# A decode block's last row: the second norm taken from moments, and the last chunks of the row before moved

## The chip, the cores and the metric

The kernel runs on one core of a Trainium2 chip. The metric is the device time of one execution in microseconds (us), as the median of several runs. A profiled execution gives a trace of every engine beside it: TensorE (PE, with its weight loads as PEld), VectorE (DVE), ScalarE (ACT), GpSimd (POOL) and SyncE (SP), which issues the transfers.

## The reference

A decode step for B = 4 rows of D = 512 channels: adaptive layer norm, cached attention with 32 query heads over 8 key heads, and a token-mixing MLP, each behind a gate.

```python
x = A_x
mod = (_silu(c) @ w_mod).reshape(c.shape[0], 6, 1, -1)
sa, ca, ga, sb, cb, gb = (mod[:, 0], mod[:, 1], mod[:, 2], mod[:, 3], mod[:, 4], mod[:, 5])
h = _layernorm(x, axis=-1) * (1 + ca) + sa
x = x + ga * _A_ref(h, A_k_cache, A_v_cache, A_wq, A_wo)   # softmax attention over 4096 cached keys
h = _layernorm(x, axis=-1) * (1 + cb) + sb
x = x + gb * _B_ref(h, B_w1, B_b1, B_w2, B_b2)

# _B_ref, with S = 1 token and F = 1792 features
h = _layernorm(x, axis=-1)
u = _gelu(jnp.einsum("bsd,sf->bdf", h, w1) + b1)
y = jnp.einsum("bdf,fs->bds", u, w2) + b2
```

So between the attention's output and the gelu of one row stand two layer norms in sequence: the modulated one, h1 = norm(x) * (1 + cb) + sb, and a second, plain norm of h1 inside `_B_ref`. Then each of 1792 features takes gelu(norm(h1) * w1 + b1), and the features are summed with w2.

## The kernel before

The 32 pairs of row and key head are worked through in order, pair i being row i // 8. Each has 2 MB of keys and 2 MB of values, which SyncE's queue loads into a ring of three 4 MB slots. For pair i `scores` multiplies, `row_max` to `expo` make the softmax's numerators, `turn` transposes them, `values` multiplies by the values, `pick` and `copy_o` bring the head's output into columns and `project` multiplies it by its part of wo. The sum over the heads is a row's attention output. The MLP of a row, class `Mixer`, runs under the attention of the next row: its 14 chunks of 128 features are expanded (`expand`, on VectorE), put through gelu on ScalarE and contracted with w2 on TensorE, two chunks at a time. A row is held in a folded form, [128 partitions, 128 columns]: partition group c of 32 holds the channels c*128 to c*128 + 127, and 8 partitions of each group belong to one row. The gates and shifts lie in `prep` in the same form.

For the last pairs the order of all steps is written out by hand in the string `PLAN`, whose words are read from left to right; each engine executes its own instructions in that order. `mix` is the MLP of row 2 there: `x` expands its next two chunks, `g` is their gelu, `c` contracts one such pair of chunks. Words with capital or small letters and a number are steps of a pair (`V29` copies the values' product of pair 29, `P28` adds the projection of pair 28, `p31` projects pair 31, `E` forms what the last row has besides its last two heads). `T2` and `T3` touch the root and the gelu on ScalarE ahead of their use, so that the function table is loaded there.

The words that begin with z are the last row's own path. Its attention output with the residual is summed in PSUM, in `pgx[:, 4]`; the mean `mu` is known shortly before. `zs` squares the centred row on ScalarE and sums it per partition, `za` (`centre`) multiplies the centred row by 1 + cb on VectorE, `zq` sums over the partitions on TensorE, `zm` (`adaln_last`) takes the root, forms h1 up to a factor and takes its statistics, `zb0` and `zb1` broadcast h1 to all partitions by matmuls, two of its four groups each, `zv` (`gather_more`) brings the statistics together, and `zn` (`affine`) takes the mean and the variance from them, the power -1/2 on GpSimd, a copy `hb` of the broadcast row less its mean on ScalarE, and the weights `wr` times the power. `zc` closes row 2's contraction, which is 512 columns wide and accumulates in four groups of partitions. `finish` then runs the last row's 14 chunks: the first two by ScalarE alone, the others expanded by VectorE, all through gelu on ScalarE and contracted on TensorE; the outputs follow.

Of the kernel before, what the change touches and what calls it, by code (L numbers as in the profile page):

```python
# [10 lines left out]
OP = mybir.AluOpType  # L11
# [17 lines left out]
def adaln_decode(ctx: ExitStack, tc: tile.TileContext, small, x, wmod, wq, kk, kv, vv, wo, out):  # L29
# [64 lines left out]
    osb = cst.tile([P, B, P], F32, name="osb")  # L94
# [95 lines left out]
    def load_wm5():  # L190
        t = slots().rearrange("p s (k n) -> p (s k) n", n=D)
        nc.sync.dma_start(t[:, 0:4], wmod[2][:, 1])
        WM[5] = t[:, 0:4]
        return t[:, 4:6]
# [178 lines left out]
    XK = cst.tile([P, B, P], F32, name="xk")  # L373
# [34 lines left out]
    def centre(x, mu):  # L408
        a = wk.tile([P, P], F32, name="a")
        dv.scalar_tensor_tensor(a, x, mu, prep[:, 3], op0=OP.add, op1=OP.mult)  # L410
        return a

    def adaln_last(b, pst, a):
        r = cst.tile([P, 1], F32, name="sd")
        h1 = wk.tile([P, P], F32, name="h1")
        nc.scalar.activation(r, pst, AF.Sqrt, bias=epsc, scale=1.0 / D)
        dv.scalar_tensor_tensor(h1, prep[:, 2], r, a, op0=OP.mult, op1=OP.add)
        pst = ps_m.tile([P, 27], F32, name="pst", tag="m")
        dv.tensor_scalar(pst[:, 24:27], eps9, r, r, op0=OP.mult, op1=OP.mult)
        return h1, stats(h1, b), pst  # L420

# [28 lines left out]
    def contract_wide(py, u, js):  # L450
        for e, j in enumerate(js):
            q = j % 4
            mm(py[32 * q:32 * q + 32, :], w2[:, j:j + 1].to_broadcast([P, 32]), u[:, e, :],  # L453
               start=(j < 4), stop=(j >= NF - 4))

    class Mixer:
# [21 lines left out]
        def gather_more(self):  # L478
            mm(self.pst[:, 0:24], ones, self.st.rearrange("p a b -> p (a b)"), start=True, stop=True)
            self.st = self.pst  # L480

        def modulate(self):
            if self.b < B - 1:
                self.h1, self.st = adaln(self.b, self.st)
            else:
                self.h1, self.st, self.pst = adaln_last(self.b, self.st, self.a)
# [26 lines left out]
        def consume(self, most=9):  # L513
            if self.py is None:
                self.py = ps_e.tile([P, D if self.wide else P], F32, name="py", tag="e")
            for u, js in self.done[:most]:
                (contract_wide if self.wide else contract)(self.py, u, js)
# [34 lines left out]
    def finish(b, pg, py, hb, wr):  # L552
        uu = ring.tile([P, 16, D], F32, name="uu", tag="kv")
        for js in ((0,), (1,), (2, 3, 4), (5, 6, 7), (8, 9, 10), (11, 12), (13,)):
# [17 lines left out]
        dv.scalar_tensor_tensor(gx, gbl, b2, XK[:, b], op0=OP.mult, op1=OP.add)  # L572
# [15 lines left out]

    def fold_gate(gate, es):
# [7 lines left out]
    mu = cst.tile([P, 1], F32, name="mu")  # L597

# [19 lines left out]
    for i in range(NS - HKV):  # L618
# [30 lines left out]
        if i == 2:  # L649
            for t in range(2, 5):  # L650
# [11 lines left out]
    mix, row = Mixer(B - 2), Mixer(B - 1)  # L662
    pve = pgx = pc = ep = spare = slot = None
# [9 lines left out]
    b31 v28.1 B31 f e31 LV31 l30 V28 L30 t30.1 l31 L31 a28 t31.1 A28 p28 v29.0 v29.1 t30.0 f P28 V29 v30.0 a29  # L673
    v30.1 A29 LW p29 f v30.2 v30.3 t31.0 P29 g V30 Y y a30 A30 p30 E x v31.0 f v31.1 v31.2 v31.3 V31 z31 a31 I A31 j p31
    g T2 zs za zx zq c c zm zb0 T3 zv zb1 zw0 zn zc
# [5 lines left out]
           "N": mix.normalise, "g": mix.gelu, "c": lambda: mix.consume(1), "zc": mix.gather_up, "zv": row.gather_more,  # L681
           "zg": row.gather,
           "zm": row.modulate, "zn": lambda: row.normalise(cst.tile([P, 1], F32, name="yl"))}
    for step in PLAN.split():
# [25 lines left out]
        elif op == "LW":  # L710
            spare = load_wm5()
        elif op == "x":
            mix.expand(spare if mix.n == 6 else None)
# [18 lines left out]
        elif step == "T3":  # L732
            nc.scalar.activation(tab, neg1, AF.Gelu_apprx_tanh)
        elif op == "zq":
            ph = ps_s.tile([P, 8, P], F32, name="ph3", tag="s")
            row.st = ph[:, 2, 0:1]
            mm(row.st, g32[:, 8 * (B - 1):8 * (B - 1) + 1].to_broadcast([P, P]), sq, start=True, stop=True)
        elif op == "zs":
            sq = cst.tile([P, 1], F32, name="sq")
            flat = wk.tile([P, P], F32, name="flat")  # L740
            nc.scalar.activation(flat, pgx[:, 4], AF.Square, bias=mu, accum_out=sq)
        elif op == "j":
            tally_up()
        elif op == "za":
            row.a = centre(pgx[:, 4], mu)
        elif op == "zx":
            dv.tensor_copy(XK[:, B - 1], pgx[:, 4])
        elif op == "zw":
            modmm(pgx[:, 0], 5, (0,))
        elif op == "zb":  # L750
            if i:
# [37 lines left out]
```

## Time and profile before

| | |
|---|---|
| time, median of 3 runs | 386.73 us (386.31 to 386.73) |
| span of the profiled execution | 384.7 us (its own time isn't listed) |
| mean granted TensorE clock | 0.883 |
| PE busy | 298.7 us, 78% |
| DVE busy | 198.2 us, 52% |
| ACT busy | 112.2 us, 29% |
| DMA, whole span | 157.69 MB, 410 GB/s |

The span runs from the first to the last instruction of the profiled execution; the time holds what lies around it as well. Busy shares are means over the whole span, so a short stretch with another limit has to be read from its own rows.

### The profile page before, as it was taken

The numbers are of one execution on the slowest core, as the hardware profiler recorded it, in microseconds if no ns is written. First come the engines' busy times: TensorE is split into PE (matmuls) and PEld (weight loads), VectorE is DVE, ScalarE is ACT, GpSimd is POOL, SyncE is SP. The second block draws the span as 40 slices with busy tenths as digits, with TensorE's granted clock in tenths as the row PEclk, the third lists the DMA queues.
The fourth block names the chain that finished last, engine by engine and source line by source line (L and its number), as shares of the span: only waits on it lengthen the run. The fifth ranks groups of instructions, "written<-read, shape, count | busy, mean of one in ns | idle before, by whom it ended". The sixth has DMA issues, their size and how long they took to land.

```text
span 384.7 us, 5604 instructions
## 1 busy us (share of the span) xinstructions
PE 298.7 (78%) x2380; PEld 117.2 (30%) x2380; DVE 198.2 (52%) x407; ACT 112.2 (29%) x144; POOL 7.7 (2%) x33
## 2 busy tenths in 40 slices
PE   0856777866966949979877878788888887999984
PEld 0112122311323313334322222342222343333653
DVE  1130251620451424664866545557665567778757
ACT  1001111121110110212567311124575105657276
POOL 1100000000000000000000000000000000000000
PEclk9989555985695685998999998999999999999999
DMA  8999999999999999999999999999999999999930
GB/s 331 433 433 436 411 453 433 409 432 436 423 441 433 434 436 436 434 436 431 429 425 433 428 433 434 429 433 431 429 434 436 434 436 432 424 417 423 418 122 3
DMA packets 7409, 157.69 MB, mean 410 GB/s; under 512 B 964, under 2 KB 1236, under 8 KB 1496
## 3 DMA queue, kind: packets, MB, share of 16 engines
q1 hardware_dynamic: 7376, 157.33, 95.4%
q8 instruction: 18, 0.29, 0.3%
q14 instruction: 7, 0.06, 0.0%
q10 hardware_dynamic: 8, 0.00, 0.0%
HBM read 157.32 MB, written 0.01 MB: 409 GB/s over the span
## 4 chain that ended last, share of the span: by engine, by line
DMA 60%; PE 29%; DVE 7%; ACT 2%; issue 1%; POOL 0%; SPq 0%; POOLq 0%; DVEq 0%
DMA kv<-in_kv 58%; PE s L231 8%; PE pv L291 7%; PE s L122 2%; PE qs L138 2%; DVE m L236 2%; DVE p L267 2%; DMA sm<-in_small 2%; PE pa L343 2%; PE pt L328 2%; ACT uu L562 1%; PE pb L251 1%; PE pve L303 1%; PE pm L240 1%; PE pgx L348 1%
## 5 line engine op out<-in xcount | busy, mean ns | idle before, releaser
L231 PE MATMUL s<-kv,QT 128*32 128x512 f32 x512 | 75.2, 714 | 38.9 <-DMA kv<-in_kv 37.0
L236 DVE TENSOR_REDUCE m<-s 128x1 f32<-128x1024 f32 x32 | 39.2, 1224 | 96.0 <-PE s L231 95.9
L261 ACT ACTIVATE p<-s,nm 128x1024 f32<-128x1024 f32 x32 | 35.7, 1115 | 180.6 <-DVE nm L256 180.5
L291 PE MATMUL pv<-kv,p 128*32 128x512 f32 x464 | 69.8, 670 | 0.7 <-DMA kv<-in_kv 0.7
L231 PEld LDWEIGHTS s<-kv,QT 128*32 128x32 f32 x512 | 15.8, 123 | 84.0 <-DMA kv<-in_kv 52.5
L328 PEld LDWEIGHTS pt<-g,po 128*128 128x128 f32 x236 | 31.1, 205 | 27.2 <-issue 19.9
L343 PE MATMUL pa<-wo,oT 128*32 128x512 f32 x240 | 34.6, 648 | 4.6 <-DVE oT L335 4.4
L328 PE MATMUL pt<-g,po 128*128 128x4 f32 (+2 forms) x236 | 33.9, 267 | 1.5 <-DVE po L314 1.0
L267 DVE STREAM_TRANSPOSE p<-p 128x1024 f32<-128x1024 f32 x25 | 30.9, 1234 | 0.0
L314 DVE COPY po<-pv 128x512 f32<-128x512 f32 x29 | 20.0, 688 | 16.8 <-PE pv L291 16.7
L245 DVE TENSOR_REDUCE mx<-pm 1x128 f32<-1x512 f32 x32 | 21.3, 669 | 1.1 <-PE pm L240 1.1
L442 DVE TENSOR_SCALAR u<-hb,wr,sm 128x512 f32<-128x512 f32 x40 | 19.9, 541 | 1.9 <-POOL wr L437 1.0
L506 ACT ACTIVATE u<-u 128x1024 f32<-128x1024 f32 x20 | 20.4, 1051 | 1.5 <-DVE u L442 1.4
L361 DVE TENSOR_TENSOR acc<-acc,pa 128x512 f32<-128x512 f32 x26 | 17.8, 686 | 4.3 <-PE pa L343 4.2
L261 ACT ACT_TABLE_LOAD x11 | 14.1, 1283 | 20.3 <-DVE nm L256 20.2
L251 PEld LDWEIGHTS pb<-neg,mx 1*128 1x128 f32 x64 | 10.4, 202 | 28.2 <-DVE mx L245 26.5
L122 PE MATMUL s<-wm,sT 128*4 128x512 f32 x16 | 9.1, 732 | 10.6 <-DVE sT L108 10.6
L506 ACT ACT_TABLE_LOAD x13 | 16.7, 1283 | 0.2
L291 PEld LDWEIGHTS pv<-kv,p 128*32 128x32 f32 x464 | 13.4, 146 | 7.2 <-issue 3.1
L240 PE MATMUL pm<-ident,m 128*1 128x128 f32 x32 | 9.3, 289 | 7.4 <-DVE m L236 3.5
L251 PE MATMUL pb<-neg,mx 1*128 1x1 f32 x64 | 13.1, 271 | 2.1 <-DVE mx L245 2.1
L453 PE MATMUL py<-u,sm 128*32 128x512 f32 x80 | 14.4, 616 | 0.0
(158 smaller groups left out, 214.7 us busy)
## 6 DMA issues: line engine op xcount, KB each, us to landing
kv<-in_kv SPq DMA_DIRECT2D x28, 4096.0 KB, 21.9
wq<-in_wq SPq DMA_DIRECT2D x2, 4096.0 KB, 16.3
wo<-in_wo SPq DMA_DIRECT2D x4, 2048.0 KB
kv<-in_kv SPq DMA_DIRECT2D x4, 2048.0 KB, 20.3
wm<-in_wmod SPq DMA_DIRECT2D x2, 2048.0 KB, 14.8
kv<-in_kk SPq DMA_DIRECT2D x1, 4096.0 KB
kv<-in_vv SPq DMA_DIRECT2D x3, 1024.0 KB
wm<-in_wmod SPq DMA_DIRECT2D x1, 1024.0 KB
```

The source lines that it names most:

```text
L231: mm(s[32 * c:32 * c + 32, n * 512:(n + 1) * 512], QT[:, b, h, :], KT[i][:, (n * 4 + c) * 512:(n * 4 + c + 1) * 512], start=True, stop=True)
L236: dv.tensor_reduce(M[i], S[i], axis=AX.X, op=OP.max)
L245: dv.tensor_reduce(mx, M[i].rearrange("o (c r) -> o r c", c=4).unsqueeze(1).to_broadcast([1, 4, 32, 4]), axis=AX.X, op=OP.max)
L251: mm(pb, M[i].rearrange("o c r -> o (c r)"), neg1, start=True, stop=True)
L261: nc.scalar.activation(p, S[i], AF.Exp, bias=M.pop(i), accum_out=l)
L267: dv.transpose(PL[i][0], PL[i][0])
L291: mm(PV[i][32 * q:32 * q + 32, :], pT[:, 128 * k:128 * k + 128:4], VT[i][:, 4 * k:4 * k + 4, :].rearrange("p j d -> p (j d)"), start=(k < ...
L314: dv.tensor_copy(PV[i], pv)
L328: mm(pt, po[:, c * DH:(c + 1) * DH], sel.unsqueeze(1).to_broadcast([P, m, REP]), start=(c == 0), stop=(c == n - 1))
L343: mm(pa[32 * g:32 * g + 32, :], oT[:, g:g + 1].to_broadcast([P, 32]), wo_t[h][:, g, :], start=True, stop=True)
L442: dv.tensor_scalar(u[:, e, :], hb, wr[:, j:j + 1], b1[:, j:j + 1], op0=OP.mult, op1=OP.add)
L506: nc.scalar.activation(u, u, AF.Gelu_apprx_tanh)
```

## The change

The last row's second norm is no longer taken from h1. With a = (x - mean) * (1 + cb) and the shift sb, h1 is a / sd + sb, so the variance of h1 follows from four sums over the row: of the squares of x - mean, of a, of a squared and of a times the centred shift. `zs` and `last_rows` sum the first two, `zp` and the second reduction of `last_rows` the other two, all into columns of one small tile `mom`; `zq` and `zv` each bring two of them to all partitions with the constant column `mid`. What depends on the shift alone is made once, early in the stream, by `spread_shift`. The broadcast `zb0`, `zb1` takes a, not h1, so it stands ahead of the root in the order; `hb` is formed behind it on VectorE from a, the root and the broadcast shift. The mean of h1 is not taken off `hb`: it goes, times w1, into the bias of the gelu (`shift`, which stands in for b1 in `finish`).

Row 2's last two pairs of chunks move: the expansion of chunks 12 and 13 and the gelus of 10 to 13 stand ahead of `V29`, beside a copy by ScalarE (`lift`) of the first ten chunks' contraction out of PSUM. In the tail `fold_rest` folds that copy and adds the last four chunks' contraction in narrow form. The last row stays in PSUM (`x1`) instead of `XK`, and `osb` takes a buffer of the pool of the chunks.

```diff
-    v30.1 A29 LW p29 f v30.2 v30.3 t31.0 P29 g V30 Y y a30 A30 p30 E x v31.0 f v31.1 v31.2 v31.3 V31 z31 a31 I A31 j p31
-    g T2 zs za zx zq c c zm zb0 T3 zv zb1 zw0 zn zc
+    b31 v28.1 B31 f e31 LV31 l30 V28 L30 t30.1 l31 L31 a28 t31.1 A28 p28 v29.0 v29.1 t30.0 f P28 g x g zy V29 v30.0 a29
+    v30.1 A29 LW p29 f v30.2 v30.3 t31.0 P29 V30 Y y a30 A30 p30 E v31.0 f v31.1 v31.2 v31.3 V31 z31 a31 I A31 j p31
+    T2 zs za zp zq zb0 zk T3 zv zb1 zn zw0 zc
...
-    eps9 = cst.tile([P, 3], F32, name="eps9")
-    nc.gpsimd.memset(eps9, 0.0)
-    nc.gpsimd.memset(eps9[:, 0:1], 1e-20)
-    nc.gpsimd.memset(eps9[:, 2:3], EPS * D)
+    mid = cst.tile([P, 1], F32, name="mid")
+    dv.tensor_scalar(mid, g32[:, 8 * (B - 1):8 * (B - 1) + 1], 1.0 / D, None, op0=OP.mult)
...
+        def lift(self):
+            self.yw = up.tile([P, 2, D], F32, name="u")[:, 0]
+            nc.scalar.activation(self.yw, self.py, AF.Copy)
+
+        def fold_rest(self):
+            py = ps_e.tile([P, P], F32, name="pc", tag="e")
+            for c in range(4):
+                mm(py[32 * c:32 * c + 32, :], g32, self.yw[:, c * P:(c + 1) * P], start=True, stop=False)
+            for u, js in self.done:
+                for e, j in enumerate(js):
+                    for c in range(4):
+                        mm(py[32 * c:32 * c + 32, :], w2[:, j:j + 1].to_broadcast([P, 32]),
+                           u[:, e, c * P:(c + 1) * P], start=False, stop=(j == NF - 1))
+            self.py = py
...
+    def spread_shift():
+        psb = ps_m.tile([P, 4, P], F32, name="psb", tag="m")
+        for c in range(4):
+            e = 32 * c + 8 * (B - 1)
+            mm(psb[:, c, :], ident[:, e:e + 1].to_broadcast([P, P]), prep[:, 2], start=True, stop=True)
+        psb = psb.rearrange("p c n -> p (c n)")
+        st = wk.tile([P, 6], F32, name="st")
+        dv.bn_stats(st, psb)
+        dv.bn_aggr(smv, st)
+        dv.tensor_scalar(sfull, psb, smv[:, 0:1], None, op0=OP.subtract)
+        dv.tensor_scalar(spart, prep[:, 2], smv[:, 0:1], 2.0, op0=OP.subtract, op1=OP.mult)
+        dv.tensor_scalar(smv[:, 1:2], smv[:, 1:2], EPS, None, op0=OP.add)
...
+    def last_rows(x):
+        al = wk.tile([P, P], F32, name="a")
+        ju = wk.tile([P, P], F32, name="flat")
+        dv.scalar_tensor_tensor(al, x, mu, prep[:, 3], op0=OP.add, op1=OP.mult, accum_out=mom[:, 1:2])
+        dv.tensor_tensor_reduce(ju, al, spart, 1.0, 0.0, OP.mult, OP.add, mom[:, 3:4])
+        return al
+
+    def squares(x, col, **kw):
+        flat = wk.tile([P, P], F32, name="h1")
+        nc.scalar.activation(flat, x, AF.Square, accum_out=mom[:, col:col + 1], **kw)
+
+    def means(dst, cols):
+        mm(dst, mid.to_broadcast([P, P]), mom[:, cols], start=True, stop=True)
+
+    def first_moments(g1):
+        nc.scalar.activation(sd, g1[:, 0:1], AF.Sqrt, bias=epsc)
+        dv.tensor_copy(momc, g1)
+        dv.tensor_scalar(kk1[:, 0:1], momc[:, 0:1], EPS, smv[:, 1:2], op0=OP.add, op1=OP.mult)
+        dv.scalar_tensor_tensor(kk1[:, 1:2], momc[:, 1:2], momc[:, 1:2], kk1[:, 0:1], op0=OP.mult, op1=OP.subtract)
+        dv.tensor_scalar(shift[:, 0], w1, momc[:, 1:2], -1.0, op0=OP.mult, op1=OP.mult)
+
+    def second_moments(g2, ab):
+        y = cst.tile([P, 1], F32, name="yl")
+        wr = wk.tile([P, NF], F32, name="wr")
+        hb = wk.tile([P, D], F32, name="hb")
+        dv.scalar_tensor_tensor(vv1[:, 0:1], g2[:, 1:2], sd, kk1[:, 1:2], op0=OP.mult, op1=OP.subtract)
+        dv.tensor_add(vv1[:, 1:2], g2[:, 0:1], vv1[:, 0:1])
+        root(vv1[:, 1:2], P, y)
+        dv.scalar_tensor_tensor(hb, sfull, sd, ab, op0=OP.mult, op1=OP.add)
+        dv.scalar_tensor_tensor(shift[:, 1], shift[:, 0], y, b1, op0=OP.mult, op1=OP.add)
+        nc.gpsimd.tensor_tensor(wr, w1, y.to_broadcast([P, NF]), op=OP.mult)
+        return hb, wr, shift[:, 1]
...
+        elif op == "zs":
+            squares(pgx[:, 4], 0, bias=mu)
+        elif op == "za":
+            al = last_rows(pgx[:, 4])
+        elif op == "zp":
+            squares(al, 2)
         elif op == "zq":
             ph = ps_s.tile([P, 8, P], F32, name="ph3", tag="s")
+            means(ph[:, 2, 0:2], slice(0, 2))
+        elif op == "zk":
+            first_moments(ph[:, 2, 0:2])
+        elif op == "zv":
+            means(ph[:, 3, 0:2], slice(2, 4))
+        elif op == "zn":
+            hb, wr, b1l = second_moments(ph[:, 3, 0:2], ph[:, 4:8].rearrange("p c n -> p (c n)"))
+            py = ps_v.tile([P, P], F32, name="py3", tag="pv")
...
+            bcast(al, B - 1, ph[:, 4 + 2 * i:6 + 2 * i], (2 * i, 2 * i + 1))
+    finish(B - 1, pgx[:, 0], py, hb, wr, b1l, pgx[:, 4])
```

## Rows read from the trace of the kernel before

**Rows 1.** The page's span in 40 slices: DMA busy tenths, GB/s.

```profile
DMA  8999999999999999999999999999999999999930
GB/s 331 433 433 436 411 453 433 409 432 436 423 441 433 434 436 436 434 436 431 429 425 433 428 433 434 429 433 431 429 434 436 434 436 432 424 417 423 418 122 3
```

**Rows 2.** Chain of waits, end: start, length in us, engine, tile, line.

```profile
370.83 0.99 PE py L453 x8
...
373.88 1.52 ACT uu L557 x2
375.40 4.12 ACT uu L562 x3
...
380.61 0.99 PE py L447 x24
```

**Rows 3.** Timeline, 369.9 to 379.5 us: start, length, engine, line, operation, [idle before].

```profile
369.94 0.37 ACT L741 ACTIVATE flat<-pgx,mu 128x128 f32<-128x128 f32 x1 [1.07 <-PE pgx L348]
370.20 0.19 ACT L741 ACTIVATION_READ_ACCUMULATOR flat<-pgx,mu 128x1 f32 x1
370.43 0.35 DVE L410 SCALAR_TENSOR_TENSOR a<-pgx,mu,prep 128x128 f32<-128x128 f32 x1 [0.77 <-ACT flat L741]
...
370.45 0.38 PE L737 MATMUL ph<-sq,g 128*128 128x1 f32 x2 [0.58 <-ACT flat L741]
...
370.87 0.26 ACT L416 ACTIVATE sd<-ph,epsc 128x1 f32<-128x1 f32 x1 [0.47 <-PE ph L737]
371.15 1.28 ACT L733 ACT_TABLE_LOAD   x1
...
371.94 0.18 DVE L380 TENSOR_TENSOR stm<-st,ident 128x24 f32<-128x24 f32 x1
372.20 0.30 PEld L479 LDWEIGHTS pst<-stm,ones 128*128 128x128 f32 x2
...
372.45 0.69 PE L427 MATMUL py<-h,ident 128*128 128x128 f32 x4
...
373.00 0.55 POOL L100 TENSOR_TENSOR yl<-mv,half 128x1 f32<-128x1 f32 x1 [54.02 <-DVE mv L396]
...
373.61 0.43 PE L366 MATMUL pc<-yw,g 128*32 128x128 f32 x8
373.63 0.21 POOL L437 TENSOR_TENSOR wr<-w1n,yl 128x14 f32<-128x14 f32 x1
...
373.89 5.57 DVE L442 TENSOR_SCALAR uu<-hb,wr,sm 128x512 f32<-128x512 f32 x12 [0.42 <-POOL wr L437]
```

**Rows 4.** Timeline, 358 to 368 us: around row 2's last chunks.

```profile
358.65 0.69 DVE L361 TENSOR_TENSOR acc<-acc,pa 128x512 f32<-128x512 f32 x1
...
360.40 0.29 DVE L314 COPY po<-pvn 128x128 f32<-128x128 f32 x1 [1.06 <-PE pvn L303]
...
364.90 0.35 DVE L726 CUSTOM_DVE_ANT_0 ep<-ep,prep,g 128x128 f32<-128x128 f32 x1
365.17 0.08 DVE L726 DVE_READ_ACCUMULATOR2_ANT tally<- 128x1 f32 x1
365.27 1.00 DVE L442 TENSOR_SCALAR kv<-hb,wr,sm 128x512 f32<-128x512 f32 x2
...
367.23 0.14 PEld L303 LDWEIGHTS pve<-kv,p 128*32 128x32 f32 x4 [0.17 <-DMA kv<-in_vv]
```

**Rows 5.** Groups by form, VectorE: line, operation, count | busy us, mean ns | idle before.

```profile
L361 DVE TENSOR_TENSOR acc<-acc,pa 128x512 f32<-128x512 f32 x26 | 17.8, 686 | 4.3 <-PE pa L343 4.2
...
L256 DVE COPY nm<-pb 128x1 f32<-128x1 f32 x32 | 5.0, 156 | 16.1 <-PE pb L251 16.0
...
L576 DVE TENSOR_TENSOR osb<-py,gbl 128x128 f32<-128x128 f32 x1 | 0.3, 292 | 0.1
```

**Rows 6.** Stretch 88 to 90 us: us, PE, PEld, DVE, ACT, POOL busy, clock, DMA.

```profile
88.00:90.00 2.00, 1.16 (x12) 0.41 (x16) 0.00 (x0) 0.67 (x2) 0.00 (x0) 0.50 0.87 377
```

**Rows 7.** Timeline, the small matmuls in that stretch.

```profile
88.44 0.66 PE L221 MATMUL pc<-ym,g 128*32 128x128 f32 x8 [0.78 <-ACT ym L218]
```

More of the change, by code (lines that the diff above doesn't have):

```diff
@@ L371, in residual @@
         dv.tensor_add(x1, x1, prep[:, 0])
-    XK = cst.tile([P, B, P], F32, name="xk")
+    XK = cst.tile([P, B - 1, P], F32, name="xk")
     ZK = cst.tile([P, B - 1, P], F32, name="zk")
@@ L453, in contract_wide @@
             mm(py[32 * q:32 * q + 32, :], w2[:, j:j + 1].to_broadcast([P, 32]), u[:, e, :],
-               start=(j < 4), stop=(j >= NF - 4))
+               start=(j < 4), stop=(last - 4 < j))
     class Mixer:
@@ L476, in gather @@
             self.pst = None
-        def gather_more(self):
-            mm(self.pst[:, 0:24], ones, self.st.rearrange("p a b -> p (a b)"), start=True, stop=True)
-            self.st = self.pst
         def modulate(self):
[L483 to L486, printed above, removed]
+            self.h1, self.st = adaln(self.b, self.st)
         def spread(self, pb=None, cs=range(4)):
@@ L516, in consume @@
             for u, js in self.done[:most]:
-                (contract_wide if self.wide else contract)(self.py, u, js)
+                if self.wide:
+                    contract_wide(self.py, u, js, NF - 1 if self.b < B - 2 else 9)
+                else:
+                    contract(self.py, u, js)
             del self.done[:most]
@@ L597, in adaln_decode @@
     mu = cst.tile([P, 1], F32, name="mu")
+    smv = cst.tile([P, 2], F32, name="smv")
+    sfull = cst.tile([P, D], F32, name="sfull")
+    spart = cst.tile([P, P], F32, name="spart")
+    mom = cst.tile([P, 4], F32, name="mom")
+    momc = cst.tile([P, 2], F32, name="momc")
+    sd = cst.tile([P, 1], F32, name="sd")
+    kk1 = cst.tile([P, 2], F32, name="kk1")
+    vv1 = cst.tile([P, 2], F32, name="vv1")
+    shift = cst.tile([P, 2, NF], F32, name="shift")
+    def last_rows(x):
[26 more added lines that the diff above has]
+        return hb, wr, shift[:, 1]
     def tally_up():
@@ L656, in adaln_decode @@
                     nc.scalar.activation(dst, pm, AF.Copy)
+        if i == 5:
+            spread_shift()
         if i == NS - HKV - 2:
             gate = spread_gate()
-    mix, row = Mixer(B - 2), Mixer(B - 1)
-    pve = pgx = pc = ep = spare = slot = None
+    mix = Mixer(B - 2)
+    pve = pgx = pc = ep = slot = None
     gates = list(range(2 * REP))
@@ L680, in adaln_decode @@
     MIX = {"F": mix.fold, "R": mix.residual, "G": mix.gather, "M": mix.modulate, "H": mix.gather, "Q": mix.spread,
-           "N": mix.normalise, "g": mix.gelu, "c": lambda: mix.consume(1), "zc": mix.gather_up, "zv": row.gather_more,
-           "zg": row.gather,
-           "zm": row.modulate, "zn": lambda: row.normalise(cst.tile([P, 1], F32, name="yl"))}
+           "N": mix.normalise, "g": mix.gelu, "c": lambda: mix.consume(1), "zy": mix.lift, "zc": mix.fold_rest, }
     for step in PLAN.split():
@@ L710, in adaln_decode @@
         elif op == "LW":
-            spare = load_wm5()
+            load_wm5()
         elif op == "x":
-            mix.expand(spare if mix.n == 6 else None)
+            mix.expand()
         elif op == "f":
@@ L750, in adaln_decode @@
         elif op == "zb":
-            if i:
-                py = ps_v.tile([P, 4, P], F32, name="py3", tag="pv")
-            row.spread(py[:, 2:4] if i else ph[:, 4:6], (2 * i, 2 * i + 1))
-    finish(B - 1, pgx[:, 0], py[:, 0], row.hb, row.wr)
+            bcast(al, B - 1, ph[:, 4 + 2 * i:6 + 2 * i], (2 * i, 2 * i + 1))
+    finish(B - 1, pgx[:, 0], py, hb, wr, b1l, pgx[:, 4])
 def kernel(**inputs):
```

44 lines of the change are left out of this document (10 added, 34 removed).

## Prediction

> **What bounds the kernel now.** I read the page's slices first. The DMA engines are full from the first slices to the one before the last two, at a nearly even rate, and then stop [rows 1]: the kernel streams the caches until about 367 us, and whatever changes before that moment is hidden as long as it neither starves the stream nor delays the work on its last piece. The span is 384.7 us, so some 17 us are a tail without transfers, and only there can this edit earn or lose time. The profiled execution has no time of its own listed; I set its span beside the median of 386.73, which leaves 2.0 us around it, and apply the shift of the span to the median.
>
> Next the chain of waits in the tail [rows 2]. From 373.88 to 381.6 it is ScalarE's gelu of the last row and the last contraction: ScalarE runs without a gap from its first gelu to its last, and VectorE's expansions start together with it [rows 2, 3]. Nothing in this stretch is changed by the edit but its start. So the question is one number: when can the first gelu of the last row start? Before, that is 373.88.
>
> Last the timeline between the end of the row's sum (pgx, about 369.9) and 373.88 [rows 3]. Before, the steps are: square and its accumulator read on ScalarE, a reduction over partitions on TensorE (`zq`), the root, `h1`, its statistics, a second reduction (`gather_more`), mean and variance, the power on GpSimd, the scaled weights, the gelu.
>
> **The change part by part.**
>
> *Ahead of the tail.* Chunk pair 12, 13 of row 2 is expanded before `V29` instead of after `E`: two instructions, 1.00 us [rows 4]. VectorE ended `P28` at 359.34 and then idled 1.06 us until it could copy `V29` at 360.40 [rows 4]; the pair fits in this gap, so I take nothing. What is queued behind it is `V29`, then `A29` and the projection. If the gap were gone the price is up to 1.00 us, less the 0.17 us that TensorE's loads wait for the last piece at 367.23 [rows 4]. Two gelus and the new copy `lift` go to ScalarE, which has nothing else until the tail. `spread_shift`, the constant `mid` and the three memsets lie where DMA is full; no queue that issues transfers waits on them for more than a fraction of a transfer, so nothing either way. No transfer is added, dropped or reordered, and SP and GpSimd's queue are not passed.
>
> *First half of the tail, a loss.* `zs` starts as before and its accumulator read ends at 370.39 [rows 3]. `za` follows at 370.43: it already stood there, with pgx long finished and ScalarE reading the same tile [rows 3]. New is that `zq` reads two sums, so it also waits for `za`'s. With the accumulator read I price `za` by the reduction with a read on the same 128x128, 0.35 and 0.08 overlapping, ending 0.35 after its start [rows 4]: 370.80 with a few hundredths for the start of the next. Below: 0.35, no read. Above: ScalarE's read, 0.19 more [rows 3]. `zq` then begins at 370.86 against 370.45 and ends at 371.24. Meanwhile `zp`, another square with its read, occupies ScalarE from 370.84 for 0.45 to 371.29, so the root `sd` starts at 371.31 and ends at 371.57, against 370.87 and 371.13: **0.44 us later**. The gelu table follows the root in both; its load of 1.28 and the small activation of about 0.2 end near 373.1 and bind nothing.
>
> *Second half, a gain.* After the root the old kernel needs 373.88 - 371.13 = 2.75 us. The new one: `momc` copies the two means out of PSUM, 0.16 by the row of a 128x1 copy [rows 5], from 371.60 to 371.76. `zv` writes into the bank that the root and `momc` read, so TensorE waits for `momc`. Its load begins at 371.83 (old: 372.20, 0.08 after the end of its input [rows 3]). `zb1` is queued behind it. In the old kernel the same pair of jobs, reduction and two broadcasts, took from 372.20 to 373.14, 0.94 us [rows 3]; so the broadcast is complete at 372.77. `hb` on VectorE, 128x512 with one operand in PSUM, is not in the trace. The add of that size is 0.686, and the three-operand form costs 0.352 against 0.292 at 128 columns [rows 3, 5], so I take 0.75: 372.81 to 373.56. Below it is 0.69, the add; above it is four times the 128-column row, 1.41. `shift` is a small instruction behind it, about 0.2, started while `hb` drains: 373.68. The first gelu starts at **373.72**.
>
> Beside it runs the branch over GpSimd. The four small instructions after `momc` are 0.16 to 0.2 each with 0.04 between (bounds: the 128x1 copy, and 0.35 of the 128-column form [rows 3, 5]); the variance stands at about 372.72, the power takes 0.55 and the weights 0.21 with 0.08 ahead of each [rows 3]: about 373.65. So the two branches end nearly together, and speeding up one alone would earn little.
>
> *The old wide contraction* (0.99 us on the chain [rows 2]) leaves the stretch between `zq` and the broadcasts. It is worth less than it looks: behind it waited broadcasts whose input was ready only after the root. `fold_rest` puts 8 and 32 small matmuls after `zw0`. By 0.43 for eight [rows 3] they take no more than 2.2 us, from about 373.2 to 375.4 at the latest. The first contraction of the last row may wait for them, but its sum is needed only at the end; `close` reads them at 379. Removing the copies of pgx and of `yw` on VectorE touches no instruction that the chain waits on.
>
> *Sum.* +0.44 for the later root, then 373.72 - 371.57 = 2.15 instead of 2.75: -0.60. Together **-0.16 us**, a span of about 384.5 us. From the median: 386.73 - 0.16 = 386.57, which I round to **386.5**. With `hb` at 0.69 and no accumulator read, and the GpSimd branch as floor, it is -0.35; with `hb` at 1.41, +0.5.
>
> *One rule against the row.* The order of `zv` behind `momc` is the dearest assumption. The row that bears on it is `za`: pgx was summed at about 369.9, ScalarE began at 369.94, and VectorE, idle, began its read of the same tile only at 370.43, as soon as ScalarE was done [rows 3]. The Trainium skill, PSUM — Partial Sum Buffer, section "PSUM bank collisions raise a hardware error", says that two engines must be kept from one bank and quadrant at the same time even at different columns. By that rule the sum above stands, and this change pays for it three times (`za` behind `zs`, `momc` behind the root, `zv` behind `momc`); without it the sum is that of the first rival.
>
> **The rivals.**
>
> *`zv` is not held.* Its columns are not those that `momc` reads. It could then go as soon as `zp`'s sum stands and `zb0` has passed, about 371.65; the broadcast is done at 372.6, `hb` at 373.38 and the gelu starts at 373.5, a time of 386.73 - 0.37 = 386.4. For it: different columns. Against it: `za`'s start [rows 3].
>
> *The sums share a tile and are taken one after another (slower).* The four columns of `mom` are written by two engines in turn. If the tile, not the column, is what is waited on, `zp` waits for VectorE's second reduction (370.80 + 0.37), and `zq` for `zp`. The root then starts at 372.14 instead of 371.31, +0.83, and the whole is +0.67: 387.4. It decides as soon as the added wait exceeds 0.16 us. Against it: ScalarE and VectorE begin to write different columns of `uu` at 373.88 and 373.89, side by side [rows 2, 3].
>
> *TensorE's clock falls in the tail.* TensorE has less to do from 369.9 to 372. Between 88 and 90 us, granted 0.50 (1.2 GHz), eight of the small matmuls took 0.66; in the tail they took 0.43 at full clock (2.4 GHz) [rows 3, 6, 7]. The last contraction, 0.99 [rows 2], would grow by half, +0.5: 386.73 - 0.16 + 0.5 = 387.1. Against it: old and new both leave a gap after pgx, and the added contraction keeps TensorE busy from 371.8 to 375.
>
> *The moved pair is in the way (slower).* If `P28` ends later, `V29` slips by up to 1.00, and with 0.17 to spare at the last piece the sum is +0.83 - 0.16: 387.4. Against it: what follows from `V29` is folded only at `y`, and the projections of pairs 30 and 31, which come last, do not read it.
>
> **How the numbers follow.** The forecast, with its own range of 386.2 to 386.9, gets 0.62. `zv` not held: 0.09. The shared tile 0.08, the clock 0.06, the moved pair 0.05. I leave 0.10 to shares that I can't see, as a different end of the stream, of either sign. A measurement of this kernel tells about 0.2% from no change, 0.77 us: below 385.96 is faster, above 387.50 slower. The forecast and all the named rivals lie inside; outside reach their edges and the unseen share. Faster 0.12, same 0.80, slower 0.08. The range takes in `zv` not held with `hb` at its cheapest and a little more below, and the shared tile above: 385.8 to 387.3, which leaves out the two dearest cases at their full price.
>
> **What would show it.** In the changed kernel: first gelu of the last row near 373.7 if the stream ends at the same moment; the root about 0.4 later than before, and `zq` starting right after `za`'s accumulator read; TensorE's load for `zv` starting right after `momc`; `hb` near 0.75; `V29` still at 360.4; a copy and two gelus on ScalarE between 357 and 363; granted clock 1.00 to the end. The prediction is wrong if the stream ends at another time, if `zp` or `zq` waits on the second reduction, if `zv` starts before `momc`, or if the stretch after the first gelu is not the 8 us that it was.

## The result, and the profile after

The changed kernel takes 387.9 us, the median of six runs (387.51 to 388.32), against 386.73 (386.31 to 387.87) for the kernel before on the same chip: a ratio of 1.0034, with a 95% interval of 1.0024 to 1.0044. It is slower by some 1.2 us where the forecast was a gain of 0.2, and it lies outside the range that I gave.

The page of the kernel after, its span and the line of the 40 slices that answers to [rows 1]:

```profile
span 386.0 us, 5673 instructions
...
DMA  8999999999999999999999999999999999999910
```

The stream is as full as before; the span has grown from 384.7 to 386.0. The profiled execution took 387.94, so what lies around the span is 1.9 us here too. The whole difference is in the span.

Where in the span? The stretch from the first gelu of the last row to the end of the last add was 8.36 us before (373.88 to 382.24; the last add, from the timeline of the kernel before, 373 to 386 us) and is 8.39 now (375.22 to 383.61, below).

```profile
381.95 0.29 DVE L577 TENSOR_TENSOR osb<-osb,a 128x128 f32<-128x128 f32 x1
```

The row's sum came 0.13 later: `zs` started at 370.07 instead of 369.94 [rows 3]. TensorE's load for the last piece of the stream was as much later, 367.38 for 367.23 [rows 4]; in three of the executions below, with the same stream, it came between 367.05 and 367.40, so I take this as scatter. What is left lies between `zs` and the first gelu. I call this **the stretch**: 369.94 to 373.88 before, 3.94 us; now 370.07 to 375.22, 5.15 us. The forecast had it at 3.78.

The timeline of the kernel after, 353 to 386 us in the first two lines and the last, 369 to 387 in the others (columns as in [rows 3]):

```profile
359.22 1.00 DVE L424 TENSOR_SCALAR u<-hb,wr,sm 128x512 f32<-128x512 f32 x2
...
360.36 0.29 DVE L310 COPY po<-pvn 128x128 f32<-128x128 f32 x1
...
370.07 0.37 ACT L624 ACTIVATE h<-pgx,mu 128x128 f32<-128x128 f32 x1 [6.72 <-PE pgx L344]
...
370.56 0.35 DVE L618 SCALAR_TENSOR_TENSOR a<-pgx,mu,prep 128x128 f32<-128x128 f32 x1 [0.77 <-ACT h L624]
370.83 0.08 DVE L618 DVE_READ_ACCUMULATOR a<-pgx,mu,prep 128x1 f32 x1
370.95 0.31 ACT L624 ACTIVATE h<-a 128x128 f32<-128x128 f32 x1 [0.43 <-DVE a L618]
...
370.97 0.38 PE L627 MATMUL ph<-mom,mid 128*128 128x2 f32 x2 [0.97 <-DVE a L618]
...
371.22 0.69 PE L409 MATMUL ph<-a,ident 128*128 128x128 f32 x4
371.95 0.26 ACT L630 ACTIVATE sd<-ph,epsc 128x1 f32<-128x1 f32 x1 [0.59 <-PE ph L409]
...
372.24 0.16 DVE L631 COPY momc<-ph 128x2 f32<-128x2 f32 x1 [0.99 <-ACT sd L630]
...
372.45 0.38 PE L627 MATMUL ph<-mom,mid 128*128 128x2 f32 x2 [0.55 <-DVE momc L631]
...
372.70 1.05 PE L409 MATMUL ph<-a,ident 128*128 128x128 f32 x4
...
373.78 0.22 DVE L640 SCALAR_TENSOR_TENSOR vv<-ph,sd,kk 128x1 f32<-128x1 f32 x1 [0.73 <-PE ph L409]
...
374.11 0.73 DVE L643 SCALAR_TENSOR_TENSOR hb<-sfull,sd,ph 128x512 f32<-128x512 f32 x1
...
375.22 1.52 ACT L550 ACTIVATE uu<-hb,shift,wr 128x512 f32<-128x512 f32 x2 [1.50 <-POOL wr L645]
...
383.32 0.29 DVE L571 TENSOR_TENSOR u<-u,a 128x128 f32<-128x128 f32 x1
```

Read it for what ends each wait. `zq` starts right behind `za`'s accumulator read, at 370.97, and is done at 371.35. The root (L630) reads nothing but `zq`'s two columns and does not start then: it starts at 371.95, and the wait of 0.59 ahead of it was ended by the matmuls of line 409, the broadcast `zb0`, which end at 371.91. The same happens below: the variance (L640) reads `zv`'s columns, done at 372.83, and starts at 373.78, behind the second broadcast `zb1`, which ends at 373.75. Neither reader uses a broadcast. They share only its tile: `zq` writes `ph[:, 2]`, `zv` `ph[:, 3]`, `zb0` and `zb1` `ph[:, 4:8]`. The trace also holds the counts (semaphores) that one engine raises and the others wait for. TensorE's rises at 371.92 and 373.76, at the ends of `zb0` and `zb1`, and at no time near 371.35: `zq` raises none of its own.

A second thing is in the length of `zb1`, 1.05 where `zb0` took 0.69. The stretches of one microsecond in the kernel after, and the first of them in the kernel before (columns as in [rows 6]):

```profile
373.00:374.00 1.00, 1.00 (x12) 0.76 (x15) 0.26 (x2) 0.71 (x2) 0.00 (x0) 0.50 0.00 0
...
375.00:376.00 1.00, 1.00 (x24) 0.94 (x20) 0.88 (x3) 0.78 (x2) 0.10 (x1) 0.50 0.00 0
```

```profile
373.00:374.00 1.00, 0.88 (x18) 0.34 (x16) 0.58 (x2) 0.92 (x3) 0.76 (x2) 1.00 0.00 0
```

TensorE's granted clock was 0.50 (1.2 GHz) from about 373 to 376, where the kernel before had 1.00 (2.4 GHz). So there were two suspects, the shared tile and the clock, and a third that the trace spoke against already: the moved chunks fit into their gap, as forecast (359.22 to 360.22, and `V29` at 360.36).

### The profile page after: what moved, and what is told of

The parts are those of the page before. It is cut to its first block, busy times and chain, and to the rows that moved or that the text cites. A ratio compares the mean times of both kernels' runs of the same rounds, so it can differ in the third digit from the quotient of the medians.

```text
span 386.0 us, 5673 instructions
## 1 busy us (share of the span) xinstructions
PE 303.0 (78%) x2412; PEld 122.3 (32%) x2412; DVE 200.7 (52%) x417; ACT 112.2 (29%) x145; POOL 7.5 (2%) x30
## 4 chain that ended last, share of the span: by engine, by line
DMA 54%; PE 34%; DVE 8%; ACT 2%; issue 1%; POOL 0%; SPq 0%; POOLq 0%; DVEq 0%
DMA kv<-in_kv 52%; PE s L227 9%; PE pv L287 9%; PE pa L339 3%; DVE m L232 3%; PE pt L324 2%; PE s L119 2%; PE qs L135 2%; DVE p L263 2%; DMA sm<-in_small 2%; PE pb L247 1%; ACT uu L555 1%; PE pve L299 1%; PE pm L236 1%; PE pgx L344 1%
## 5 line engine op out<-in xcount | busy, mean ns | idle before, releaser
L287 PE MATMUL pv<-kv,p 128*32 128x512 f32 x464 | 71.3, 684 | 0.6 <-DMA kv<-in_kv 0.6
L324 PEld LDWEIGHTS pt<-g,po 128*128 128x128 f32 x236 | 32.7, 214 | 27.8 <-issue 18.0
L339 PE MATMUL pa<-wo,oT 128*32 128x512 f32 x240 | 36.3, 679 | 4.1 <-DVE oT L331 4.0
L324 PE MATMUL pt<-g,po 128*128 128x4 f32 (+2 forms) x236 | 35.5, 274 | 1.5 <-DVE po L310 1.0
L481 ACT ACTIVATE u<-u 128x1024 f32<-128x1024 f32 x21 | 21.4, 1051 | 3.8 <-DVE u L424 3.7
L424 DVE TENSOR_SCALAR u<-hb,wr,sm 128x512 f32<-128x512 f32 x42 | 20.9, 540 | 1.9 <-POOL wr L419 1.0
L236 PEld LDWEIGHTS pm<-ident,m 128*1 128x1 f32 x32 | 2.5, 79 | 37.8 <-DVE rl L276 27.4
```

The costliest lines, as they stand in the source:

```text
L287: mm(PV[i][32 * q:32 * q + 32, :], pT[:, 128 * k:128 * k + 128:4], VT[i][:, 4 * k:4 * k + 4, :].rearrange("p j d -> p (j d)"), start=(k < ...
L324: mm(pt, po[:, c * DH:(c + 1) * DH], sel.unsqueeze(1).to_broadcast([P, m, REP]), start=(c == 0), stop=(c == n - 1))
L339: mm(pa[32 * g:32 * g + 32, :], oT[:, g:g + 1].to_broadcast([P, 32]), wo_t[h][:, g, :], start=True, stop=True)
L481: nc.scalar.activation(u, u, AF.Gelu_apprx_tanh)
```

## The experiments

All kernels but one start from the changed kernel; the kernel before ran on the same chips, with medians of 386.48 to 386.52. On one of them (the kernels with only the first and only the second result apart, the short fillers and the shorter second half) its times scattered, from 386.33 to 391.25 about a median of 386.48. That pulls the ratios there down and widens their intervals, so for these kernels I go by the medians.

**Own tiles for both results.** `zq`'s and `zv`'s means go into PSUM tiles of their own; the broadcasts keep `ph`.

```diff
-            means(ph[:, 2, 0:2], slice(0, 2))
+            g1 = ps_m.tile([P, 2], F32, name="g1", tag="m")
+            means(g1, slice(0, 2))
...
-            first_moments(ph[:, 2, 0:2])
+            first_moments(g1)
...
-            means(ph[:, 3, 0:2], slice(2, 4))
+            g2 = ps_m.tile([P, 2], F32, name="g2", tag="m")
+            means(g2, slice(2, 4))
...
-            hb, wr, b1l = second_moments(ph[:, 3, 0:2], ph[:, 4:8].rearrange("p c n -> p (c n)"))
+            hb, wr, b1l = second_moments(g2, ph[:, 4:8].rearrange("p c n -> p (c n)"))
```

> The changed kernel with the two reductions' results in two PSUM tiles of their own; the broadcasts keep theirs. Measure: from the start of the first square (zs) to the first gelu of the last row, 3.94 us before the change and 5.15 after it. Tile theory (the root and the variance wait for the broadcasts because all four write one tile): the root starts 0.05 after zq's matmul instead of 0.60, the variance no longer waits for zb1, the stretch falls to about 3.8, the time by 1.3 to about 386.6. Clock theory (TensorE fell to 1.2 GHz and that is the loss): the root still waits, the stretch stays at 4.8 to 5.15. Moved-chunks theory (the loss lies ahead of the row's sum): the stretch shortens but the time stays above 387.5.

386.52 us, a ratio of 0.9998 (0.9989 to 1.0007). Its timeline, 369.8 to 375.3 us:

```profile
370.12 0.37 ACT L624 ACTIVATE h<-pgx,mu 128x128 f32<-128x128 f32 x1 [6.55 <-PE pgx L344]
...
371.03 0.38 PE L627 MATMUL g<-mom,mid 128*128 128x2 f32 x2 [0.97 <-DVE a L618]
...
371.45 0.26 ACT L630 ACTIVATE sd<-g,epsc 128x1 f32<-128x1 f32 x1
371.69 0.30 PEld L627 LDWEIGHTS g<-mom,mid 128*128 128x128 f32 x2
...
371.74 0.16 DVE L631 COPY momc<-g 128x2 f32<-128x2 f32 x1 [0.43 <-ACT sd L630]
...
371.94 0.69 PE L409 MATMUL ph<-a,ident 128*128 128x128 f32 x4
...
372.51 0.22 DVE L640 SCALAR_TENSOR_TENSOR vv<-g,sd,kk 128x1 f32<-128x1 f32 x1
...
373.95 1.52 ACT L550 ACTIVATE uu<-hb,shift,wr 128x512 f32<-128x512 f32 x2 [0.73 <-POOL wr L645]
```

The root now starts right behind `zq` (371.03 + 0.38), which raises a count of its own at 371.42, while `zb0` is still running; the variance starts behind small instructions of its own engine, while `zb1` (371.94 + 0.69) is running. The stretch is 3.83 us, and the clock stayed at 1.00. The whole loss is gone with the tile, so the moved chunks and the new sums are not its cause. But `zv` has also come loose from `momc`, the order that I had called my dearest assumption, so this run alone does not say which of the waits counted.

**One own tile for both results.** `zq` and `zv` share a tile, apart from the broadcasts, so `zv` must still wait for `momc`.

```diff
-            means(ph[:, 2, 0:2], slice(0, 2))
+            gg = ps_m.tile([P, 2, 2], F32, name="gg", tag="m")
+            means(gg[:, 0], slice(0, 2))
...
-            means(ph[:, 3, 0:2], slice(2, 4))
+            means(gg[:, 1], slice(2, 4))
```

> As the run with own tiles, but both reductions share one PSUM tile, apart from the broadcasts; so zv must still wait for momc, as the prediction had it. Tile theory: root 0.05 after zq, stretch 3.8 to 3.95, because the chain of small instructions on VectorE to the variance, not zv, ends last. If zv behind momc is dear, the stretch is 0.4 longer than with own tiles. Clock theory: as with own tiles.

386.42 us, 1.0001 (0.9985 to 1.0016), a stretch of 3.82. Its timeline, 369.2 to 377 us:

```profile
369.88 0.37 ACT L624 ACTIVATE h<-pgx,mu 128x128 f32<-128x128 f32 x1 [6.71 <-PE pgx L344]
...
371.71 0.30 PEld L627 LDWEIGHTS gg<-mom,mid 128*128 128x128 f32 x2 [0.18 <-DVE momc L631]
...
373.70 1.52 ACT L550 ACTIVATE uu<-hb,shift,wr 128x512 f32<-128x512 f32 x2 [0.72 <-POOL wr L645]
```

`zv`'s weight load starts at 371.71, right behind `momc` (0.18 of idle, ended by it), and it costs nothing. What I had weighed most carefully does not matter; the wait for the broadcasts does.

**Only the first, only the second result apart.** In the first kernel `zq`'s means alone have their own tile (`g1` of the first edit), in the second `zv`'s alone (`g2`).

```diff
+            means(g1, slice(0, 2))
...
+            first_moments(g1)
```

```diff
+            means(g2, slice(2, 4))
...
+            hb, wr, b1l = second_moments(g2, ph[:, 4:8].rearrange("p c n -> p (c n)"))
```

> The changed kernel with only zq's result in a tile of its own; zv's stays with the broadcasts. Tile theory: the root starts right after zq (the loss of 0.55 there is gone), the variance still waits for zb1, which now ends about 0.15 after the small instructions on VectorE are done: stretch 3.95 to 4.0, time 386.6. If the two waits cost alike, it is half way, 4.5.

> The changed kernel with only zv's result in a tile of its own; zq's stays with the broadcasts. Tile theory: the root still starts 0.60 after zq, behind zb0, and all small instructions behind it are as late; the variance does not wait for zb1: stretch 4.3 to 4.4, time 387.0. Clock theory: if TensorE stays busy enough to keep 2.4 GHz the stretch is near 4.

With the first apart 386.64 us, 0.9992 (0.9967 to 1.0017). The timeline of that kernel, 369.8 to 375.3 us:

```profile
369.98 0.37 ACT L624 ACTIVATE h<-pgx,mu 128x128 f32<-128x128 f32 x1 [6.39 <-PE pgx L344]
...
371.80 0.69 PE L409 MATMUL ph<-a,ident 128*128 128x128 f32 x4
...
372.18 0.23 DVE L634 TENSOR_SCALAR shift<-sm,momc 128x14 f32<-128x14 f32 x1
...
372.53 0.22 DVE L640 SCALAR_TENSOR_TENSOR vv<-ph,sd,kk 128x1 f32<-128x1 f32 x1
...
373.97 1.52 ACT L550 ACTIVATE uu<-hb,shift,wr 128x512 f32<-128x512 f32 x2 [0.89 <-POOL wr L645]
```

The stretch is 3.99 us: most of the loss is gone. The variance still reads from `ph`, and still starts right behind `zb1` (371.80 + 0.69), 0.12 after its own engine was free. It costs little now, because with the root early `zb1` is early too.

With the second apart 386.96 us (386.82 to 387.37), the time that was expected, 0.48 above the median of the kernel before; its ratio, 0.9991 (0.9962 to 1.0019), suffers from the scatter named above. The profiled execution was its slowest, with a stretch of 4.96, and shows why, in the timeline, 369.2 to 376.2 us, and in the stretch from 371 to 372 us:

```profile
369.83 0.37 ACT L624 ACTIVATE h<-pgx,mu 128x128 f32<-128x128 f32 x1 [6.55 <-PE pgx L344]
...
370.98 1.03 PE L409 MATMUL ph<-a,ident 128*128 128x128 f32 x4
...
372.05 0.26 ACT L630 ACTIVATE sd<-ph,epsc 128x1 f32<-128x1 f32 x1 [0.93 <-PE ph L409]
...
372.56 1.22 PE L409 MATMUL ph<-a,ident 128*128 128x128 f32 x4 [0.33 <-DVE momc L631]
...
374.79 1.52 ACT L550 ACTIVATE uu<-hb,shift,wr 128x512 f32<-128x512 f32 x2 [0.97 <-POOL wr L645]
```

```profile
371.00:372.00 1.00, 1.00 (x8) 1.00 (x7) 0.01 (x2) 0.12 (x2) 0.00 (x0) 0.59 0.00 0
```

The root waits for `zb0` again, and here the clock fell while `zb0` ran, so the wait grew from 0.59 to 0.93. `zb1` took 1.22 at the low clock, and `hb` waited 0.29 for it. This trace also shows the tile's wait in the other direction: `zb1` writes `ph[:, 6:8]`, and it had to wait for `momc`, which reads `ph[:, 2]`.

What one own tile is worth depends on the order in which they are given: `zq`'s first takes most of the loss (to 386.64), `zv`'s first some half of it (to 386.96).

**The changed kernel once more.** The same program in one more execution, for the clock.

> The changed kernel once more, one look. Tells whether the fall of TensorE's clock in the tail belongs to it or to one execution: if it falls again between 372 and 374, zb1 takes about 1.05 and the stretch is 5.1 to 5.2; if not, 0.7 and 4.8.

387.52 us, span 385.6. The timeline, 369.8 to 375.3 us, and the stretch from 373 to 374 us:

```profile
369.99 0.37 ACT L624 ACTIVATE h<-pgx,mu 128x128 f32<-128x128 f32 x1 [6.70 <-PE pgx L344]
...
371.87 0.26 ACT L630 ACTIVATE sd<-ph,epsc 128x1 f32<-128x1 f32 x1 [0.59 <-PE ph L409]
...
372.62 0.69 PE L409 MATMUL ph<-a,ident 128*128 128x128 f32 x4
...
373.35 0.22 DVE L640 SCALAR_TENSOR_TENSOR vv<-ph,sd,kk 128x1 f32<-128x1 f32 x1 [0.38 <-PE ph L409]
...
374.80 0.81 ACT L550 ACTIVATE uu<-hb,shift,wr 128x512 f32<-128x512 f32 x1 [1.15 <-POOL wr L645]
```

```profile
373.00:374.00 1.00, 1.00 (x31) 0.88 (x34) 0.61 (x3) 0.64 (x2) 0.15 (x1) 1.00 0.00 0
```

The clock stayed at 1.00, `zb1` took 0.69, and both waits for the broadcasts are there as before. The stretch is 4.81. So the waits alone make the kernel slower, and the fall of the clock belongs to an execution, not to the program: the first one, in which it fell, has 0.34 more (5.15), and its `zb1` is 0.36 longer.

**TensorE kept busy.** Two kernels add matmuls to the changed kernel whose results nobody reads, ahead of `zq` and behind `zb0`. The first adds five of 512 columns, all into the same 32 partitions; the second four side by side in four groups of partitions, of 384 and then 160 columns.

```diff
+    def fill(n):
+        pf = ps_m.tile([P, D], F32, name="pf", tag="m")
+        for _ in range(n):
+            mm(pf[0:32, :], g32, sfull, start=True, stop=True)
...
+    T2 zs za zp zf3 zq zb0 zf2 zk T3 zv zb1 zn zw0 zc
```

```diff
+    def fill(n):
+        pf = ps_m.tile([P, D], F32, name="pf", tag="m")
+        for c in range(4):
+            mm(pf[32 * c:32 * c + 32, 0:8 * n], g32, sfull[:, 0:8 * n], start=True, stop=True)
...
-    T2 zs za zp zq zb0 zk T3 zv zb1 zn zw0 zc
+    T2 zs za zp zf48 zq zb0 zf20 zk T3 zv zb1 zn zw0 zc
```

> The changed kernel with five wide matmuls added whose result nobody reads, three ahead of zq and two behind zb0, to keep TensorE at work; waits unchanged. Tile theory with the clock as a second part: granted clock 1.00 through the tail, zb1 0.7 instead of 1.05, first gelu 0.35 earlier (stretch 4.8), time 387.5. Clock theory: the stretch falls to about 4 and the time to 386.7. If the clock costs nothing, no change from 387.9.

> The changed kernel, waits unchanged, with narrower unread matmuls in the two gaps: four of 384 columns side by side ahead of zq (about 0.85 us in the gap of 0.97) and four of 160 behind zb0 (about 0.45 in the gap of 0.54). Tile theory with the clock as a part of the loss: granted clock 1.00, zb1 0.7 instead of 1.05, stretch from zs to the first gelu 4.8 instead of 5.15, time 387.5. Clock theory (the clock is most of the loss): stretch about 4. If the clock costs nothing: 5.15.

The first missed: 390.22 us, 1.0097 (1.0083 to 1.0110). I had sized the fillers by matmuls that run side by side; into the same partitions each pass started about 0.43 us after the one before (six of them took 2.74), and `zq` could only start at 372.50. It says nothing on the loss. The second took 387.49 us, 1.0012 (0.9988 to 1.0036), a stretch of 4.80 with the clock at 1.00; the root's wait for `zb0` was still 0.59 and the variance's for `zb1` still 0.38. That is the same as the repeat above: with the clock held, the waits and their cost stay.

**The chunks alone, the norm alone.** The kernel before with only row 2's chunks moved; and the changed kernel with own tiles and the old place of the chunks, their wide contraction standing ahead of `zq`, where TensorE waits anyway.

```diff
-    ... P28 V29 v30.0 a29 ... P29 g V30 ... E x v31.0 ...
-    g T2 zs za zx zq c c zm zb0 T3 zv zb1 zw0 zn zc
+    ... P28 g x g zy V29 v30.0 a29 ... P29 V30 ... E v31.0 ...
+    T2 zs za zx zq zm zb0 T3 zv zb1 zw0 zn zc
```

```diff
-    ... P28 g x g zy V29 v30.0 a29 ... P29 V30 ... E v31.0 ...
-    T2 zs za zp zq zb0 zk T3 zv zb1 zn zw0 zc
+    ... P28 V29 v30.0 a29 ... P29 g V30 ... E x v31.0 ...
+    g T2 zs za zp c c zq zb0 zk T3 zy zv zb1 zn zw0 zc
```

> The kernel before with only row 2's last chunks moved (expansion, gelus and the copy ahead of V29, the narrow rest in the tail), the old norm kept. Tile theory: no loss here, stretch 3.9 to 4.0 and the time within 0.3 of before. Clock theory: without the wide contraction TensorE falls to 1.2 GHz in the tail; broadcasts and reductions then cost 0.3 to 0.6 more and the time is that much above before. Moved-chunks theory: 0.5 to 1.2 above before.

> Own tiles for both reductions, but row 2's last chunks where they were before: expansion after E, gelu ahead of T2, the wide contraction ahead of zq in the gap in which TensorE waits, the copy by ScalarE behind the gelu's table. Tells what the moved chunks are worth beside the new norm. If they are worth nothing: stretch 3.8 and 386.5, as with own tiles. If the wide contraction delays zq, or the copy the first gelu, 0.1 to 0.5 more. Clock theory: with the gap filled the granted clock is 1.00 in every execution, so fewer of the runs lie 0.4 above the others.

The chunks alone: 386.69 us, 1.0009 (1.0000 to 1.0018), a stretch of 4.05 in an execution in which the clock fell to 0.50 shortly before 373. The norm alone: 386.71 us, 1.0004 (0.9996 to 1.0013), a stretch of 3.82, with VectorE's first expansion 0.20 behind the first gelu (the next experiment has more of the same). I had expected the clock to stay at 1.00 there, with the gap filled; it did up to the first gelu, and fell to 0.50 behind it, with 0.74 as the mean from 374 to 376 and 0.50 from 376 to 378. So each half of the change, freed of the shared tile, is worth nothing that can be measured, and neither is the cause of the loss.

**A shorter second half.** With own tiles the first gelu waits for the branch over GpSimd. Here `momc` is copied first, the root is taken from the copy beside the small instructions, and the bias' first part moves behind the variance.

```diff
     def first_moments(g1):
-        nc.scalar.activation(sd, g1[:, 0:1], AF.Sqrt, bias=epsc)
         dv.tensor_copy(momc, g1)
+        nc.scalar.activation(sd, momc[:, 0:1], AF.Sqrt, bias=epsc)
...
-        dv.tensor_scalar(shift[:, 0], w1, momc[:, 1:2], -1.0, op0=OP.mult, op1=OP.mult)
```

> Own tiles for both reductions, and two changes of order: momc is copied first and the root is taken from the copy, so that VectorE's small instructions run beside the root and not behind it; the bias's first factor is formed after the variance. Theory that the chain root, momc, small instructions, power, weights is what ends last (own tiles: 3.82): the variance stands about 0.35 earlier, until hb and the bias behind it bind; stretch 3.5, time 0.35 below own tiles, 386.15. Rival: hb binds at once, behind zb1, and the stretch stays at 3.75 to 3.8.

386.54 us, 0.9984 (0.9962 to 1.0005). The first gelu came as expected, 3.56 after `zs`, and the time did not follow. The timeline of that kernel, 369.7 to 375.6 us:

```profile
373.49 1.52 ACT L550 ACTIVATE uu<-hb,shift,wr 128x512 f32<-128x512 f32 x2 [0.24 <-POOL wr L645]
373.90 1.92 DVE L424 TENSOR_SCALAR uu<-hb,wr,shift 128x512 f32<-128x512 f32 x4 [0.49 <-DVE shift L644]
...
375.39 1.49 ACT L555 ACTIVATE uu<-uu 128x1536 f32<-128x1536 f32 x1 [0.38 <-DVE uu L424]
```

VectorE's first expansion starts 0.41 after the gelu, with nothing late that it reads, and ScalarE idles 0.38 ahead of its third gelu. Ahead of the expansion on VectorE's queue stand four semaphore instructions, its waits for what used `uu`'s slot of the ring before. I took these for the cause. The last kernel takes them early: `uu` is allocated ahead of `zs`, and VectorE writes one unread column of it there.

```diff
+            uu = ring.tile([P, 16, D], F32, name="uu", tag="kv")
+            dv.memset(uu[:, 15, 0:1], 0.0)
...
-    finish(B - 1, pgx[:, 0], py, hb, wr, b1l, pgx[:, 4])
+    finish(B - 1, pgx[:, 0], py, hb, wr, b1l, pgx[:, 4], uu)
```

> The run with the root aside, and the buffer of the last row's chunks taken earlier: VectorE clears one unused column of it ahead of the row's sum. In the run with the root aside the first gelu started after 3.56, but VectorE's first expansion only 0.49 after the bias, and ScalarE then waited 0.38 for it. Theory that the waits for the buffer's seven transfer queues stand in VectorE's queue there: the first expansion starts within 0.1 of the bias, ScalarE runs without a gap, stretch 3.55, time 0.35 below the run with the root aside, 386.15, a ratio of 0.9990 to before. Rival: the expansion waits for the weights from GpSimd, and nothing changes from 386.5.

386.08 us, the median of twelve runs (385.93 to 386.18, and one of 387.64), against 386.52 before: 0.9992 (0.9983 to 1.0000). Its timeline, 369.7 to 375.6 us:

```profile
369.78 0.06 DVE L784 MEMSET uu<- 128x1 f32 x1 [0.18 <-DMA kv<-in_wmod]
369.88 0.37 ACT L623 ACTIVATE h<-pgx,mu 128x128 f32<-128x128 f32 x1 [6.55 <-PE pgx L344]
...
373.44 1.52 ACT L549 ACTIVATE uu<-hb,shift,wr 128x512 f32<-128x512 f32 x2 [0.23 <-POOL wr L644]
373.47 2.38 DVE L424 TENSOR_SCALAR uu<-hb,wr,shift 128x512 f32<-128x512 f32 x5
...
374.96 1.49 ACT L554 ACTIVATE uu<-uu 128x1536 f32<-128x1536 f32 x1
```

The expansion starts with the gelu again, and ScalarE runs without a gap. This is the best version, 0.44 us below the median of the kernel before. That is under the 0.77 us that I took a measurement here to tell from no change, but eleven of the twelve runs lie below every run of the kernel before beside them (386.32 to 386.70).

That the waits for the slot were the cause is not shown, and the traces speak against it as the whole of it. In the kernel with the late expansion the four semaphore instructions took 0.05 each and were over at 373.48; the expansion came 0.42 later. In the kernel with own tiles the same four stand there, and the expansion starts 0.05 behind the last. In the kernel with the norm alone VectorE stops for 0.41 too, but between two of its semaphore instructions. In both kernels the stop lies between the 447th and the 448th instruction of VectorE's trace. In the kernel with own tiles VectorE is busy with the expansions at that place, and in the last kernel the bias and a wait for it stand there. So the added write may have helped by taking the waits early or only by moving the queue on, and no run here separates the two.

## Why the prediction was wrong

The stretch splits into four numbers, each a difference of two rows above. Before it was 3.94. The new norm, with every wait for its own result only, is 3.83: **-0.11**, where my sum said -0.16. The shared tile adds **+0.98** (4.81 - 3.83): 0.82 of it goes when `zq`'s result has its own tile (4.81 to 3.99), 0.16 more when `zv`'s then has one too. The clock's fall adds **+0.34** (5.15 - 4.81) in the profiled execution. Without the fall 386.73 - 0.11 + 0.98 is 387.6, near the repeat's 387.52; with it, it is 387.9, as in the profiled execution (387.94) and the median. Whether the clock fell in the other five runs no trace shows.

**The step that failed** is "`zq` ... ends at 371.24 ... so the root `sd` starts" right behind it and `zp`, and with it the later one that puts the variance at 372.72. I took the readers to wait for the columns that they read. They wait for the last matmul issued so far into the tile: the root 0.56 longer than with its own tile (0.98 from `zq`'s start instead of 0.42), and the variance, at full clock, 0.41 longer behind `momc` (1.18 instead of 0.77). The edit that put the broadcast ahead of the root in the order put it ahead of the root in this wait too.

**The sign of it stood in the trace.** In [rows 3] the second reduction writes `pst`, the first broadcast `ph` and the second `py`, three tiles, and the root came before anything else was queued into `ph`. One line of the kernel before that I did not draw on, from the timeline of 371.5 to 373.95 us, is the reader of the second reduction:

```profile
372.64 0.28 DVE L396 BATCH_NORM_AGGREGATE mv<-pst 128x2 f32<-128x27 f32 x1 [0.52 <-PE pst L479]
```

It started while the broadcast into `py` was still running (372.45 + 0.69): another tile, no wait. The diff folds the three into `ph3`. I did have a rival of sums that share a tile, but asked it only of `mom`; there it was wrong, as `zp` started at 370.95, together with VectorE's second reduction, and did not wait for it. The evidence that I gave against it, `uu` written by two engines side by side, is about writers, and about SBUF; it says nothing of a reader behind matmuls.

**Weighed too heavily:** `zv` behind `momc`. It was so in the changed kernel (372.45, right behind the copy). The Trainium skill (PSUM — Partial Sum Buffer, section "PSUM bank collisions raise a hardware error") asks that different engines be kept apart by bank and quadrant, not by address. The trace agrees, there and with `za` behind `zs` at 370.56. But with this wait or without it the stretch is 3.82 or 3.83. The wait that cost the time is another one, for the broadcasts' `ph[:, 4:8]`, of which neither the root nor the variance reads a column.

**The clock** I had as a rival at 0.06 and +0.5, placed on the last contraction. It fell in the profiled execution, but on `zb1`, which had by then come onto the path. What lets it fall is not settled: in the kernel with only the first result apart and in the one with only the second, TensorE's work up to `zb0` was nearly the same, and the clock fell in one.

**What held:** the moved pair in its gap, with `V29` at 360.36; no wait of `zp` on VectorE; `zq` at the end of `za`'s read (0.90 after the start of `zs`, for 0.92 by my sum); `hb` at 0.73 for my 0.75; the stretch after the first gelu; the branch over GpSimd as the floor once the broadcasts are not waited for (0.73 of idle ahead of the gelu in the kernel with own tiles, ended by `wr`). The small instructions between `momc` and the variance were 0.16 to 0.23 each, a little dearer than I took them, and they are five, not four: I had left out the bias' first part. They follow each other so closely that the variance stood 1.02 after `momc` in the kernel with own tiles, for 0.96 by my sum. Two slips in the sums change nothing: 386.57 rounds to 386.6, and the low end of -0.35 comes to about -0.31 from its own terms (0.07 down to the floor, at most 0.08 for the read). All that held is together worth 0.1 us; one wait that I did not ask about was worth 1.

## What to carry to other kernels

Here a reader of a PSUM tile waits for the last matmul issued into that tile before it, whichever columns that writes, and a matmul into the tile waits for the readers queued before it, so a small result that is read early should have its own tile; moving work ahead of a reader in the order only helps if the two share none. When an edit merges several tiles into one, list for each reader every write that is queued into the tile ahead of it, and price the wait by the last one. And when a path gets shorter, look at whether its successor starts with its operands: here an expansion started 0.49 us after the last of them, and a write of one column, early in the queue, brought 0.46 us (386.54 to 386.08), by a cause that is not settled.

## What the runs showed that I had not expected

- The same program ran the tail once with the clock at 1.00 throughout and once with 0.50 for three microseconds, and its stretch was 4.81 and 5.15.
- Matmuls of 512 columns into the same 32 partitions followed each other at about 0.43 us a pass; eight passes of that width in four groups of partitions took 0.99 together [rows 2].
- VectorE stood still for 0.42 us between waits that were over and an instruction whose operands were ready.
